# Weights of the dynamic convolution prepared in parts that fit the groups: what a new first part, new part borders and another order of the scratch rows do

## The chip, the cores and the metric

One NeuronCore of one Trainium2 chip runs the whole program. The metric is the device time of one execution in microseconds (us). The compute engines are named as in the profile: PE (TensorE), DVE (VectorE), ACT (ScalarE), POOL (GpSimd, which here mostly issues DMAs), and SP (SyncE, which only issues DMAs).

## The reference

```
# x [8, 4224, 192], weight_gen [8, 4224, 8 heads, 7 taps]; all float32
w   = softmax(weight_gen, axis=-1)                         # 7 weights for each row and head
y   = sum over k of w[b, s, h, k] * x_pad[b, s + k, h, :]  # 6 zero rows ahead of x, 24 channels a head
g   = sigmoid(sum over j of conv_w[j] * y_pad[:, s + j])   # depthwise convolution, 5 taps
out = (g * (y @ w_val)) @ w_out                            # 192 x 192 each
```

The first line of sums is a convolution whose weights differ for every row; the rest is a gated projection of its result.

## The kernel before

**Groups and pairs.** The 4224 rows of the sequence are cut into groups of 120 rows (the first has 88, the last 56). A group holds the rows of all 8 batch lanes. Pair 0 is the first group alone, pairs 1 to 17 are two groups each, pair 18 is the last group alone. Counting groups from 0, pair 1 is groups 1 and 2, pair 2 groups 3 and 4, pair 3 groups 5 and 6.

**The dynamic convolution as matmuls.** For a group, `bank` multiplies a tile `xt` (windows of 14 rows of x on the partitions) with a tile `tb`, in which the softmax weights stand as a band along a diagonal. There are two `tb` and three `xt` buffers, used in turn. The 128 PE instructions at line 343 are one group's band matmuls. ACT copies the result from PSUM (`evac`), and POOL moves pieces of it into the ring tiles by 12 small DMAs a pair (`move`).

**How the band gets into `tb`.** The softmax weights are computed in *parts* (class `Softmax`): a part of R rows per partition covers 32 R rows of all lanes. DVE and ACT run `max`, `sub`, `exp`, `sum`, `recip`, `norm` on it. `halo` then copies the 6 rows that follow each partition's own from a neighbour partition by DMA, `spread` (four copies) writes the weights in the form of band rows, and `store` writes these to a scratch buffer z in DRAM (two buffers, `zb`, used in turn). `load_t` reads z back with a row stride that is one step short, which puts the rows on a diagonal: nine DMAs for a group of 120 rows, one for each window of 14 rows. What a row of z holds outside its weights must be zero; `clear_z` writes those zeros.

**The gate and the projections.** `tap0` (ACT) and four `tap` for each of two channel groups (DVE, line 388) are the depthwise convolution; `sigm` (ACT), `wvm_`, `wva_`, `wvd_`, `wvb_` (PE) the value projection, `gv` (DVE, line 439 and on) the gating, `omA`, `omB` (PE) the output projection, `oev` (ACT) and `store` (SP) the output. On PE the band matmuls of pair q stand between the value projection of pair q-1 and the output projection of pair q-2. The band matmuls use PSUM tiles that `gv` of the pair before must first have read.

**What sets the order.** Every step is put into a list with a planned time (`at`); the list is sorted by that time and each engine gets its steps in that order. The planned times only order the steps. `WHEN` holds the planned starts of pairs 0 to 3, `TP` the planned distance of later pairs. Waits between engines are added from what each step reads and writes. A DMA on SP or ACT carries one of eight semaphores in turn, one on POOL one of eight others; a DMA waits until the one before it with the same semaphore has landed, so at most eight of each kind are under way.

**Parts before.** `USES` lists, for each of 11 parts, the first row for which it is used and its R:

```
USES = ((0, 4, NBL), (96, 10, NBL), (364, 8, NBL), (576, RM, NBL), (1070, RM, NBL), (1564, RM, NBL), (2058, RM, NBL),
        (2552, RM, NBL), (3046, RM, NBL), (3540, RM, NBL), (4034, 8, NBL))
```

The first part serves the first group, the second nearly all of pair 1. A group whose rows cross a border takes some windows from one part and the others from the next (`segments`).

## Time and profile before

| | |
|---|---|
| median of 3 runs (range) | 536.34 us (532.11 to 536.66) |
| the profiled execution: its own time | 530.59 us |
| its span, first to last instruction | 528.8 us |
| PE, DVE, ACT, POOL busy in the span | 454.5, 427.1, 313.6, 317.3 us |
| mean granted TensorE clock | 0.942 |
| DMA traffic | 112.42 MB, mean 213 GB/s |

The durations below come from the profiled execution; 1.79 us of its own time lie outside the span. Its own time is 5.75 us under the median of the three runs, so a sum made in the trace has to be moved by that much to stand beside the median. The first 110 us are start-up, in which PE mostly waits; after them PE is busy nearly without a break until the last two pairs.

### The profile page before, as it was taken

Reading aid. Unit: us, or ns where it says so; the run is one execution under the profiler, and the core shown is the slowest. Engines: PE = TensorE matmul, PEld = TensorE weight load, DVE = VectorE, ACT = ScalarE, POOL = GpSimd, SP = SyncE. Lnnn points to the kernel's source line nnn. Section 1 sums busy time; section 2 is a strip of 40 time slices with the busy share of each in tenths; the row PEclk is TensorE's granted clock in tenths of the full one; section 3 lists DMA queues with packets and bytes.
Section 4 is the critical chain, followed back from the end, with each engine's and each line's share of the span. In section 5 each row is a group of like instructions: output and inputs, shape, how many; then the busy total and the mean of one; then the engine's idle time right before and its main releaser. Section 6 shows DMA issues by size and latency. Waiting matters only on the chain.

```text
span 528.8 us, 15980 instructions
## 1 busy us (share of the span) xinstructions
PE 454.5 (86%) x6546; PEld 330.2 (62%) x6546; DVE 427.1 (81%) x342; ACT 313.6 (59%) x433; POOL 317.3 (60%) x554
## 2 busy tenths in 40 slices
PE   7030674969999899999999999999998999999996
PEld 3030552556858485858676776768584868586584
DVE  6988346898979896999799979888995979595960
ACT  6432364658585748485858675767767575545532
POOL 9878256667474839293949382938566565807400
PEclk9565697879999999999999999999999999999999
DMA  7796749986979797879797978797797858654344
GB/s 222 212 307 187 202 110 254 244 234 175 248 218 281 196 270 195 270 195 269 208 288 201 267 199 263 202 259 220 219 254 220 256 149 251 177 165 100 92 113 111
DMA packets 86743, 112.42 MB, mean 213 GB/s; under 512 B 19133, under 2 KB 73796, under 8 KB 86542
## 3 DMA queue, kind: packets, MB, share of 16 engines
q1 hardware_dynamic: 62988, 70.86, 46.9%
q0 software_dynamic: 22560, 38.13, 28.1%
q10 hardware_dynamic: 1122, 2.40, 1.4%
q8 instruction: 52, 0.85, 0.6%
q14 instruction: 21, 0.17, 0.1%
HBM read 59.63 MB, written 42.43 MB: 193 GB/s over the span
## 4 chain that ended last, share of the span: by engine, by line
PE 44%; issue 15%; DMA 14%; POOL 13%; DVE 7%; ACT 5%; SPq 2%; ACTq 0%; POOLq 0%; DVEq 0%
PE ps L343 15%; PE ps L455 10%; POOL xt L286 6%; PE ps L464 6%; PE ps L420 5%; POOL ringA L366 4%; DMA xt<-in_x_dram 3%; PE ps L415 3%; PE ps L432 3%; POOL ringB L368 2%; DMA ringA<-S 2%; DMA tb<-z 2%; DMA ringB<-S 2%; PE ps L426 2%; DVE aB L447 1%
## 5 line engine op out<-in xcount | busy, mean ns | idle before, releaser
L343 PE MATMUL ps<-tb,xt 126*32 126x120 f32 (+2 forms) x4608 | 148.0, 286 | 62.3 <-DMA tb<-z 26.8
L343 PEld LDWEIGHTS ps<-tb,xt 126*32 126x32 f32 x4608 | 134.9, 115 | 74.5 <-issue 33.4
L388 DVE SCALAR_TENSOR_TENSOR aA<-ringA,wf,aA 128x1920 f32<-128x1920 f32 (+2 forms) x76 | 157.3, 2070 | 15.9 <-ACT aA L384 13.7
L286 POOL DMA_DIRECT2D xt<-in_x_dram x272 | 158.4, 597 | 17.8 <-DMA xt<-in_x_dram 5.0
L368 POOL DMA_DIRECT2D ringB<-S x76 | 42.1, 559 | 139.0 <-ACT ringB L358 113.0
L455 PE MATMUL ps<-wf,aA 128*120 128x192 f32 (+2 forms) x576 | 108.7, 336 | 5.9 <-DVE aB L447 3.9
L455 PEld LDWEIGHTS ps<-wf,aA 128*120 128x120 f32 (+2 forms) x576 | 91.2, 186 | 20.2 <-DVE aB L447 9.0
L470 ACT COPY ot<-ps 120x768 f32<-120x768 f32 (+2 forms) x72 | 56.0, 802 | 66.2 <-PE ps L464 55.2
L366 POOL DMA_DIRECT2D ringA<-S x152 | 82.0, 547 | 21.6 <-DMA ringB<-S 9.0
L388 DVE SCALAR_TENSOR_TENSOR aB<-ringB,wf,aB 128x960 f32<-128x960 f32 (+2 forms) x76 | 86.9, 1143 | 1.9
L439 DVE TENSOR_TENSOR aA<-ps,aA 128x960 f32<-128x960 f32 (+2 forms) x36 | 39.3, 1130 | 52.7 <-PE ps L432 33.1
L420 PE MATMUL ps<-ringA,wva 128*128 128x480 f32 (+2 forms) x144 | 61.8, 571 | 0.0
L464 PE MATMUL ps<-wf,aB 64*120 64x192 f32 (+2 forms) x576 | 59.7, 335 | 0.9 <-ACT ot L470 0.9
L358 ACT COPY S<-ps 128x480 f32<-128x480 f32 (+2 forms) x36 | 19.9, 552 | 63.2 <-PE ps L343 46.5
L464 PEld LDWEIGHTS ps<-wf,aB 64*120 64x120 f32 (+2 forms) x576 | 46.5, 182 | 16.8 <-issue 15.2
L358 ACT COPY ringA<-ps 128x480 f32<-128x480 f32 (+2 forms) x72 | 36.2, 554 | 33.7 <-PE ps L343 33.7
L384 ACT ACTIVATE aA<-ringA,wf 128x960 f32<-128x960 f32 (+2 forms) x38 | 39.2, 1033 | 22.9 <-DMA ringA<-S 22.7
L420 PEld LDWEIGHTS ps<-ringA,wva 128*128 128x128 f32 x144 | 25.8, 189 | 35.7 <-issue 22.2
L261 ACT COPY zt<-wt 128x512 f32<-128x512 f32 (+3 forms) x36 | 30.9, 936 | 5.7 <-DMA wt<-wt 3.2
L432 PE MATMUL ps<-ringB,wvb 64*128 64x480 f32 (+2 forms) x144 | 33.5, 581 | 0.0
L415 PE MATMUL ps<-ringA,wvm 128*32 128x480 f32 (+2 forms) x304 | 33.5, 537 | 0.0
L393 ACT ACTIVATE aA<-aA 128x1920 f32<-128x1920 f32 (+2 forms) x19 | 32.1, 1690 | 1.0 <-DVE aA L388 0.9
(62 smaller groups left out, 361.1 us busy)
## 6 DMA issues: line engine op xcount, KB each, us to landing
xt<-in_x_dram POOLq DMA_DIRECT2D x272, 94.5 KB, 3.7
out_dram<-ot SPq DMA_DIRECT2D x68, 360.0 KB
tb<-z SPq DMA_DIRECT2D x235, 74.4 KB
z<-zt SPq DMA_DIRECT2D x28, 306.0 KB
wt<-in_weight_gen_dram SPq DMA_DIRECT2D x28, 224.0 KB
ringA<-S POOLq DMA_DIRECT2D x136, 30.0 KB, 3.5
tb<-z SPq DMA_DIRECT2D x69, 52.1 KB
wt<-wt SPq DMA_DIRECT2D x9, 294.0 KB
```

Source lines behind the costliest of these rows:

```text
L286: eng.dma_start(out=self.xb[0:G * NW, j, 0:D], in_=src)
L343: nc.tensor.matmul(out=pa[Q * c:Q * c + Q, n * l:n * l + n], lhsT=g.xb[0:k, LH * u + l, C * h:C * h + Q], rhs=t[:, (LH * u + l) // LQ, PAD ...
L358: nc.scalar.copy(out=dst, in_=pa)
L366: nc.gpsimd.dma_start(out=ringA[q:q + h, LH * u:LH * u + LH, p0:p0 + n], in_=St[p:p + h, :, 0:n])
L368: nc.gpsimd.dma_start(out=ringB[HD * u + q:HD * u + q + h, :, p0:p0 + n], in_=St[p:p + h, :, 0:n])
L388: nc.vector.scalar_tensor_tensor(out=a, in0=self.src(g, j), scalar=cw[:, g, j:j + 1], in1=a, op0=ALU.mult, op1=ALU.add)
L415: nc.tensor.matmul(out=ps[2][c:c + Q, i, 0:self.w * self.pieces // 2], lhsT=wvm[:, Q * k:Q * k + Q], rhs=self.half(0, u, i), start=True, s ...
L420: nc.tensor.matmul(out=self.v01(e)[:, u], lhsT=wva, rhs=self.A(e, u), start=True, stop=False)
L432: nc.tensor.matmul(out=self.v01(e)[:, u], lhsT=wvb[hs], rhs=self.Bt(e)[hs], start=False, stop=True, tile_position=(HD * u, 0))
L455: nc.tensor.matmul(out=ps[b][0:n, u, D * t:D * t + D], lhsT=g[:, u, t], rhs=woa, start=first and t == 0, stop=not first, skip_group_check= ...
L464: nc.tensor.matmul(out=ps[b][0:n, u, D * t:D * t + D], lhsT=g[hs, t], rhs=wob[hs], start=first and t == 0, stop=not first, skip_group_chec ...
L470: nc.scalar.copy(out=ots[0:n, 2 * e + k], in_=ps[b][0:n, :, 0:2 * D])
```

## The change

1. The first group has 80 rows and the last 64; groups between keep 120, and there are as many pairs.
2. The parts have other borders: `(0, 10), (314, 8), (554, 8)`, then seven parts of R = 16 that start at 794 and lie 480 apart, then `(4154, 6)`. Each but the first starts six rows (`PAD`) ahead of the first row of a pair, so both groups of a pair read one part, and `load_t` is issued by windows alone.
3. The first part now has R = 10 and reads its six following rows from DRAM itself, so that it needs no `halo`; it covers groups 0, 1 and 2. Its softmax is done in two halves of 8 rows per partition.
4. z holds for each row the band rows of the four lane pairs one after the other (before: all rows of a lane pair, then the next lane pair). `store` and `load_t` get other strides; the pieces that they move stay 612 bytes and up to 1360 bytes. A row that is stored is 612 bytes in all parts (before: the first two parts stored rows of 1428 bytes, zeros included).
5. `clear_z` zeroes only the 816 bytes behind the weights, in one DMA for all lanes; there are four such DMAs, all on SP.
6. The weights of a part are loaded by one DMA instead of four.
7. Of the copies of `spread`, DVE makes two in each of the first two parts. Conversions and DMAs of the projection weights come earlier.
8. The start-up table is written anew: groups 0, 1 and 2 follow each other on PE, `WHEN` is other, and `tap0` of pair 0 comes after the last `evac` of pair 1 on ACT.

```diff
-    N0, NZ = 88, 56
+    N0, NZ = 80, 64
...
-    def clear_z(i, lo, p, n, eng):
+    def clear_z(i, lo, hi, eng):
...
+        t, n = zb[i], NL * (hi - lo) // 16
+        dst = bass.AP(tensor=t.tensor, offset=t.offset + NL * lo * PITCH + DATA,
+                      ap=[[n * PITCH, 16], [PITCH, n], [1, PITCH - DATA]])
...
+        def load(self, eng, lo=0, hi=None):
+            R, n = self.R, (hi or self.m) - lo
+            src = bass.AP(tensor=wg.tensor, offset=wg.offset + (self.r0 + lo) * ROW,
+                          ap=[[R * ROW, NBL], [LQ * S * ROW, NL], [S * ROW, LQ], [1, n * ROW]])
...
-                dst = bass.AP(tensor=t.tensor, offset=t.offset + ROWS * u * PITCH,
-                              ap=[[R * PITCH, p], [PITCH, R], [1, self.row]])
+                dst = bass.AP(tensor=t.tensor, offset=t.offset + u * PITCH,
+                              ap=[[R * NL * PITCH, p], [NL * PITCH, R], [1, self.row]])
...
-            off = (self.s - PAD + lo - p.r0) * PITCH + HC2 + skip * CELL - HC2 * i0
+            off = (self.s - PAD + lo - p.r0) * NL * PITCH + HC2 + skip * CELL - HC2 * i0
             src = bass.AP(tensor=b.tensor, offset=b.offset + off,
-                          ap=[[PITCH - HC2, hi - lo], [ROWS * PITCH, NL], [1, cells * CELL]])
+                          ap=[[NL * PITCH - HC2, hi - lo], [PITCH, NL], [1, cells * CELL]])
...
+    USES = ((0, 10, NBL), (314, 8, NBL), (554, 8, NBL), *((794 + 480 * i, RM, NBL) for i in range(7)), (4154, 6, NBL))
...
-    WHEN = (25.0, 40.0, 52.0, 70.0)
+    WHEN = (25.0, 30.0, 54.0, 79.0)
...
+    steps(s0, "max sub exp", 4.1, *h0)
+    steps(s0, "max sub exp", 4.2, *h1)
+    steps(s0, "sum recip norm", 4.3, *h0)
+    steps(s0, "sum recip norm", 4.4, *h1)
...
+    at(29.5, s3.load, SP)
...
+    steps(s3, "max sub", 44.0)
+    spread(s2, 45.0)
...
+    at(46.9, s3.exp)
```

**DVE at the start.** First before, then now, with the semaphores that each step waits for; `wt_65` holds the weights of the first part, `mx_68` its maxima and sums, DMAHW names DMAs of SP and ACT.

```order
L215 TENSOR_REDUCE mx_68<-wt_65 128x160 [waits DMAHW2_49,DMAHW3_49,DMAHW1_49,DMAHW0_49]
L219 TENSOR_TENSOR wt_65<-wt_65,mx_68 128x1120 [waits DVE_49]
L227 TENSOR_REDUCE mx_68<-wt_65 128x160 [waits Activation_49]
L231 TENSOR_SCALAR mx_68<-mx_68 128x160 [waits DVE_49]
L232 RECIPROCAL mx_68<-mx_68 128x160 [waits DVE_49]
L249 TENSOR_TENSOR wt_65<-wt_65,mx_68 128x1120 [waits DVE_49]
L215 TENSOR_REDUCE mx_69<-wt_66 128x160 [waits DMAHW6_49,DMAHW5_49,DMAHW7_49,DMAHW4_49,Pool_49]
```

```order
L215 TENSOR_REDUCE mx_68<-wt_65 128x2x64 [waits DMAHW1_49,DMAHW0_49]
L219 TENSOR_TENSOR wt_65<-wt_65,mx_68 128x2x448 [waits DVE_49]
L215 TENSOR_REDUCE mx_68<-wt_65 128x2x64 [waits Activation_49]
L219 TENSOR_TENSOR wt_65<-wt_65,mx_68 128x2x448 [waits DVE_49]
L227 TENSOR_REDUCE mx_68<-wt_65 128x2x64 [waits Activation_49]
L231 TENSOR_SCALAR mx_68<-mx_68 128x2x64 [waits DVE_49]
L232 RECIPROCAL mx_68<-mx_68 128x2x64 [waits DVE_49]
L236 TENSOR_TENSOR wt_65<-wt_65,mx_68 128x2x448 [waits DVE_49]
```

The first step waits for the loads of both halves, and the second half's maximum waits for ACT, which at that point has only the first half's `exp` to finish.

**SP from the zeroing of z to the loads of the second group.** First before, then now; `z_97` and `z_98` are the two scratch buffers, `tb_64` and `tb_63` the band tiles of groups 0 and 1 (and `tb_64` again of group 2).

```order
L181 DMA z_97<-zero 128x1x357 x4
L272 DMA z_97<-aA 32x1428 x2
L317 DMA tb_64<-z_97 8x4x238
L317 DMA tb_64<-z_97 14x4x340 x2
L317 DMA tb_64<-z_97 10x4x170
L206 DMA wt_65<-in_weight_gen_dram 32x2x896 x4
L272 DMA z_98<-aA 32x3570 x2
L241 DMA wt_67<-wt_67 112x2x336
L241 DMA wt_67<-wt_67 12x2x336
L317 DMA tb_63<-z_97 14x4x238
L272 DMA z_97<-zt 256x1x153 x4
L317 DMA tb_63<-z_98 14x4x340 x3
```

```order
L180 DMA z_97<-zero 1280x1x204
L205 DMA wt_67<-in_weight_gen_dram 128x2x448
L180 DMA z_98<-zero 1024x1x204
L272 DMA z_97<-aA 320x1x153 x2
L313 DMA tb_64<-z_97 8x4x238
L313 DMA tb_64<-z_97 14x4x340 x2
L313 DMA tb_64<-z_97 2x4x34
L313 DMA tb_63<-z_97 14x4x238
L313 DMA tb_63<-z_97 14x4x340 x3
L313 DMA tb_63<-z_97 14x4x238
L272 DMA z_98<-aA 256x1x153 x4
```

Between the loads of group 0 and those of group 1 stood the load of the fourth part, the stores of the second and third and a halo; now nothing stands there, and the second part's store comes behind group 1's loads.

**SP ahead of the loads of pair 3** (its first group's are the last rows of each, into `tb_63`). First before, then now.

```order
L317 DMA tb_64<-z_97 14x4x238
L272 DMA z_98<-zt 512x1x153 x4
L206 DMA wt_66<-in_weight_gen_dram 32x2x896 x4
L478 DMA out_dram<-ot 44x2x384 x2
L317 DMA tb_63<-z_97 14x4x238
L317 DMA tb_63<-z_98 14x4x340 x7
L317 DMA tb_63<-z_98 14x4x238
```

```order
L205 DMA wt_66<-in_weight_gen_dram 128x2x896
L272 DMA z_97<-zt 256x1x153 x4
L180 DMA z_98<-zero 1024x1x204
L245 DMA wt_65<-wt_65 112x2x336
L245 DMA wt_65<-wt_65 12x2x336
L474 DMA out_dram<-ot 40x2x384 x2
L313 DMA tb_63<-z_97 14x4x238
L313 DMA tb_63<-z_97 14x4x340 x7
```

The two halo DMAs of the fourth part (`wt_65`) now stand ahead of pair 3's loads, and with them the wait for that part's `norm` on DVE; they stood far ahead of these before.

## Rows read from the trace of the kernel before

**Rows 1.** Windows, core 0: us, busy of PE, PEld, DVE, ACT, POOL, clock, DMA share, GB/s.

```profile
0.00:110.65 110.65, 50.83 (x787) 36.09 (x787) 78.77 (x83) 51.34 (x77) 76.71 (x129) 0.75 0.80 216
110.65:528.80 418.15, 403.66 (x5760) 294.14 (x5760) 348.33 (x260) 262.28 (x357) 240.62 (x425) 0.99 0.76 212
...
139.00:463.00 324.00, 314.51 (x4605) 228.64 (x4597) 282.34 (x204) 214.29 (x287) 201.13 (x356) 1.00 0.83 231
```

**Rows 2.** Timeline of PE, start-up: start, us, engine, line, operation; band matmuls of groups 0, 1, 3, 5.

```profile
29.74 4.65 PE L343 MATMUL ps<-tb,xt 126*32 126x88 f32 x128 [19.13 <-DMA ot<-cd]
56.34 5.98 PE L343 MATMUL ps<-tb,xt 126*32 126x120 f32 x128 [21.96 <-DMA tb<-z]
...
75.13 3.88 PE L343 MATMUL ps<-tb,xt 126*32 126x120 f32 x128 [1.11 <-DVE aA L439]
...
110.65 6.06 PE L343 MATMUL ps<-tb,xt 126*32 126x120 f32 x128 [4.81 <-DMA tb<-z]
```

**Rows 3.** Timeline of SP, start-up: loads of z, halo, output, loads of z.

```profile
21.55 3.44 SPq L317 DMA_DIRECT2D tb<-z  x4
...
57.06 4.04 SPq L241 DMA_DIRECT2D wt<-wt  x2
...
86.60 1.66 SPq L478 DMA_DIRECT2D out_dram<-ot  x2
...
89.36 20.68 SPq L317 DMA_DIRECT2D tb<-z  x18
```

**Rows 4.** Timeline of DVE, first 32 us: first part's first and last step, third part's tensor_scalar.

```profile
5.63 1.32 DVE L215 TENSOR_REDUCE mx<-wt 128x160 f32<-128x1120 f32 x1 [2.70 <-DMA wt<-in_weight_gen_dram]
...
12.33 1.32 DVE L249 TENSOR_TENSOR wt<-wt,mx 128x1120 f32<-128x1120 f32 x1
...
28.34 3.52 DVE L231 TENSOR_SCALAR mx<-mx 128x128 f32<-128x128 f32 x1
```

**Rows 5.** Groups by line and form, 0 to 110.6 us: softmax steps on 896 elements.

```profile
L219 DVE TENSOR_TENSOR wt<-wt,mx 128x896 f32<-128x896 f32 x1 | 1.1, 1086 | 0.0
...
L232 DVE RECIPROCAL mx<-mx 128x128 f32<-128x128 f32 x1 | 1.0, 952 | 0.0
L223 ACT ACTIVATE wt<-wt 128x896 f32<-128x896 f32 x1 | 0.9, 949 | 5.5 <-DMA tb<-z 5.5
```

**Rows 6.** Timeline of POOL, 27 to 32 us: memsets.

```profile
27.76 1.94 POOL L511 MEMSET tb<- 128x2142 f32 x1
29.58 2.20 POOL L578 MEMSET zt<- 128x2448 f32 x1
```

**Rows 7.** Timeline of ACT, 62 to 100 us: tap0 of pair 0, a spread, an exp.

```profile
62.82 1.06 ACT L384 ACTIVATE aA<-ringA,wf 128x352 f32<-128x352 f32 x2
...
64.39 3.85 ACT L261 COPY zt<-wt 128x512 f32<-128x512 f32 x4
...
97.00 1.28 ACT L223 ACT_TABLE_LOAD   x1
98.69 1.70 ACT L223 ACTIVATE wt<-wt 128x1792 f32<-128x1792 f32 x1 [0.40 <-DVE wt L219]
```

**Rows 8.** Timeline of DVE, 82 to 128 us: taps, a part's last steps, gating.

```profile
82.00 8.98 DVE L388 SCALAR_TENSOR_TENSOR aA<-ringA,wf,aA 128x1920 f32<-128x1920 f32 x4 [5.96 <-ACT aA L384]
...
102.21 2.01 DVE L227 TENSOR_REDUCE mx<-wt 128x256 f32<-128x1792 f32 x1
...
104.59 1.75 DVE L232 RECIPROCAL mx<-mx 128x256 f32<-128x256 f32 x1
106.37 2.02 DVE L249 TENSOR_TENSOR wt<-wt,mx 128x1792 f32<-128x1792 f32 x1
...
109.44 2.21 DVE L439 TENSOR_TENSOR aA<-ps,aA 128x960 f32<-128x960 f32 x2
...
122.51 4.97 DVE L388 SCALAR_TENSOR_TENSOR aB<-ringB,wf,aB 128x960 f32<-128x960 f32 x4
```

**Rows 9.** Timeline of PE: band matmuls of the last group.

```profile
489.56 1.96 PE L343 MATMUL ps<-tb,xt 126*32 126x56 f32 x128
```

More of the change, by code (lines that the diff above doesn't have):

```diff
@@ L547, in tile_dynconv_gated_moe @@
-    tail(s1, 1.1)
-    tail(s2, 1.1)
-    steps(s0, "max sub exp", 4.1)
-    at(4.5, lambda: A.copy(out=s1.z, in_=zero[:, 0:1].unsqueeze(2).broadcast_to([P, s1.R, PITCH])))
-    steps(s0, "sum recip norm", 5.0)
-    at(7.0, clear_z, 0, 128, 16, 8, SP)
-    steps(s1, "max sub", 8.3)
-    at(8.5, s2.max)
-    at(10.0, gr[1].load_x, G_)
-    spread(s0, 11.0)
-    at(11.1, s0.store, (A, SP))
-    at(12.1, s1.exp)
-    steps(s1, "sum recip norm", 12.2)
-    at(12.3, lambda: clear(tb[0], 0, 0, CELLS, A))
@@ L572, in tile_dynconv_gated_moe @@
-    at(19.6, lambda: clear(tb[0], 2, 0, CELLS, G_))
-    at(20.0, s1.halo, (G_, G_))
-    at(20.5, load_weights)
-    spread(s1, 24.0)
-    at(24.5, s1.store, (A, SP))
-    at(24.6, lambda: clear(tb[0], 3, 0, CELLS, G_))
-    at(24.7, lambda: G_.memset(zt, 0.0))
-    tail(s3, 24.8)
-    at(24.9, s2.halo, (SP,))
-    steps(s3, "max sub", 26.0)
-    at(28.4, s3.exp)
-    steps(s3, "sum recip norm", 28.5)
-    at(29.5, gr[2].load_x, G_)
-    spread(s2, 30.0)
-    at(31.0, s2.store, (SP,))
+    at(0.2, s1.load, SP)
@@ new lines, in tile_dynconv_gated_moe @@
+    at(5.5, clear_z, 1, 0, 256, SP)
+    steps(s0, "max sub exp", 4.1, *h0)
+    steps(s0, "max sub exp", 4.2, *h1)
+    steps(s0, "sum recip norm", 4.3, *h0)
+    steps(s0, "sum recip norm", 4.4, *h1)
+    tb_clear(1, 2, 8.0, A, 0, cs)
+    tb_clear(1, 3, 8.1, A, 0, cs)
+    spread(s0, 11.0, (A, V, A, V))
+    at(11.1, s0.store, (SP, A))
+    tb_clear(0, 2, 11.5, A)
+    steps(s1, "max sub exp", 12.0)
+    tb_clear(0, 3, 12.1, A)
+    for u in range(NL):
+        tb_clear(1, u, 12.05 if u < 2 else 12.3, V, cs)
@@ L593, in tile_dynconv_gated_moe @@
-    spread(s3, 43.0)
-    for i, f in enumerate(place_weights()):
-        at(44.0 + 0.01 * i, f)
-    at(43.5, clear_z, 1, 320, 16, 12, G_)
-    load(s4, 51.0, (SP,))
-    at(50.0, s3.store, (SP,))
-    s0.ready, s1.ready, s2.ready, s3.ready = 12.0, 24.5, 31.0, 50.5
-    at(54.0, clear_z, 0, 256, 16, 16, G_)
-    steps(s4, "max sub exp", 62.0)
-    steps(s4, "sum recip norm", 66.0)
-    for p in parts[3:]:
-        q = next(q.q for q in pairs if p.use < q.s + q.n)
-        if p is s3:
-            assert q == 3
-            continue
-        if p is not s4:
-            for u in range(NL):
-                at(when(q - 5) + 12.5, p.load, u, SP)
+            at((14.0, 28.0, 29.0)[k] + 0.01 * i, lambda f=f: f(V))
@@ new lines, in tile_dynconv_gated_moe @@
+    for gi, t in enumerate((20.5, 24.0, 29.0)):
+        for w, lo, hi in gr[gi].windows():
+            at(t + 0.01 * w, gr[gi].load_t, s0, w, lo, hi, (SP, A)[w % 2])
+    spread(s1, 24.9, (A, A, V, V))
+    at(28.5, s1.store, (SP,))
+    tail(s3, 26.0)
+    at(37.0, lambda: G_.memset(zt, 0.0))
+    at(29.5, s3.load, SP)
+    steps(s2, "max sub", 32.5)
+    for i, f in enumerate(place_weights()):
+        at(33.35 + 0.001 * i, f)
+    at(32.6, s2.exp)
+    steps(s2, "sum recip norm", 32.7)
+    at(33.0, s2.halo, (G_,))
@@ L612, in tile_dynconv_gated_moe @@
+    steps(s3, "max sub", 44.0)
+    spread(s2, 45.0)
+    at(46.0, s2.store, (SP,))
+    tail(parts[4], 46.5)
+    tail(parts[5], 46.6)
+    at(46.9, s3.exp)
+    at(47.0, clear_z, 1, 256, 512, SP)
+    at(when(3) + 7.5, clear_z, 0, 320, 512, SP)
+    steps(s3, "sum recip norm", when(1) + 20.6)
+    for p in parts[3:]:
+        q = part.index(p)
+        if p is not s3:
+            at(when(q - 5) + 12.5, p.load, SP)
             for i, f in enumerate((p.max, p.sub)):
@@ L618, in tile_dynconv_gated_moe @@
         spread(p, when(q - 2) + 8.0)
-        p.ready = when(q - 2) + 12.0
-        at(p.ready, p.store, (SP,))
+        at(when(q - 2) + 12.0, p.store, (SP,))
     for q, pr in enumerate(pairs + [None, None]):
```

175 lines of the change are left out of this document (79 added, 96 removed).

## The prediction

> **What bounds the kernel now.** I read the windows first. From 110.65 us to the end PE is busy 403.66 of 418.15 us at a granted clock of 0.99; up to there it is busy 50.83 of 110.65 [rows 1]. So from the first band matmul of group 5 (pair 3) on, PE sets the pace, and ahead of it something else does. Pair 3 starts at 110.65 and the last group's matmuls at 489.56 [rows 2, 9], fifteen pairs in 378.9 us, 25.3 us a pair, and nothing in the change takes work off PE there. What can move the end is the time T3 at which pair 3 starts on PE. The PE order up to that point is the same in both kernels, so what PE has left after T3 is the same too, but for the cut of the last group.
>
> The PE timeline then shows where the 110 us went: group 0 starts at 29.74, group 1 only at 56.34, group 3 at 75.13, group 5 at 110.65 [rows 2]. The waits stand at the row ends: group 1 waited 21.96 us for `tb<-z`, group 5 another 4.81 us. Start-up is a chain of softmax, store to z, load from z, matmul, paid for several small parts one after the other.
>
> **The change, part by part.** I follow the new chain with the old durations.
>
> *First part to group 0.* Before, DVE starts when 573 KB of weights have landed, at 5.63 [rows 4]. Now it waits for both halves, 917 KB; the extra 344 KB cost between nothing (the same row) and 1.6 us at the 216 GB/s of start-up [rows 1]: I take 6.5. The halves do not overlap, because DVE waits for ACT's `exp` between them (the order of the change shows it). `max` and `sub` cost 1.09 us each for 896 elements, `exp` 0.95 [rows 5]: 2 x 3.13 = 6.3, to 12.8. Then twice `sum` 1.09, the small tensor_scalar with its gap 0.37 (102.21 + 2.01 to 104.59), reciprocal 0.95, `norm` 1.09 [rows 5, 8]: 7.0, to 19.8. Before, the first part's `norm` ended at 13.65 and the first load of `tb` was issued at 21.55 [rows 3, 4], 7.9 us for spread, store and landing; the new store has 783 KB instead of 731 and two of its four copies on DVE, so I keep 7.9: 27.7. From that issue to group 0 on PE passed 8.19 us (21.55 to 29.74) over seven loads on two queues; there are seven now: **group 0 at 35.9**, 6.2 us later than before. The zeroing of z (1.0 and 0.8 MB) is issued ahead of this store on the same queue; all that DMA has to move by then is some 5.4 MB, 25 us at 216 GB/s, so it just fits under the 22 us of softmax and spread and the landing that follows; without that cover each MB costs 4.6 us. That is the largest unknown of this step: 0 to 4 us.
>
> *Groups 1 and 2.* They read the same part, so their loads follow directly. PE needs 4.65 x 80/88 = 4.2 for group 0, to 40.1. Group 1's nine loads go out on two queues behind group 0's and can all have landed some 5 us after group 0's (five issues at 0.86 each [rows 3], 4 more if the eight semaphores hold them up). I take **group 1 at 40.5**, 16 us ahead of before. A band of 120 rows takes 3.88 us at the high clock and 5.98 at the low one [rows 2]; I take 5.5, to 46. Group 2 reuses the tile that group 0 frees at 40.1: five issues, 4.3, and the 4.7 that lay between the last issue's end (24.99) and the matmul (29.74) [rows 2, 3]: 49.1, and 5 us of matmul, **to 54**.
>
> *Pair 2.* `tap0` of pair 0 now comes after all four `evac` of group 2 on ACT, which end 1 us after the matmuls, at 55. From that `tap0` to group 3 on PE passed 75.13 - 62.82 = 12.31 us, of which 3.85 were a `spread` that stood between [rows 2, 7]: 8.5 remain. **Group 3 at 63.5**, 11.6 ahead of before.
>
> *Pair 3.* `gv` of pair 0 takes DVE until 64.5, `max` and `sub` of the fourth part 2 x 2.02, to 68.6. ACT meanwhile has `tap0` of pair 1 (3.2), the third part's spread (2.4) and a table load of 1.28 [rows 7], and ends that part's `exp` (1.70) at 71.6. `sum` to `norm` take 102.21 to 108.39, 6.2 [rows 8]: 77.8. Only then come the taps of pair 1 on DVE, 8.98 and 4.97 [rows 8], to 91.7, and the first `gv`, half of 2.21, frees the PSUM tile that group 5 needs: 92.8. On SP the fourth part's halo waits for the same `norm`; behind it stand two halo issues (1.6 to 4.0), two output issues (1.66) and nine loads (18 took 20.68 with their waits, so 7.5 to 10.3) [rows 3], and some 3 us of landing: 91.6 to 96.8. Both chains end at the same place. I take **T3 = 93.0**, 17.7 ahead. By bytes the same comes out: the DMAs that must be through by then hold some 19.9 MB (summed over the new program's order), and 216 GB/s moves that in 92 us.
>
> *After T3.* The loads by one DMA instead of four take three issues off SP for every part, and a group no longer mixes parts; it had nine loads either way, since the old borders fell on window borders. SP waits were not what PE lost after 110.65, so I cost this at nothing; if I am wrong it can give back at most the 14.5 us that PE was idle there [rows 1]. The last group of 64 rows instead of 56 costs 1.96 x 8/56 = 0.3 in band matmuls [rows 9] and about as much in its projections: 0.6.
>
> *A rule of the skill that speaks against it.* The third part's tensor_scalar took 3.52 us where the same step elsewhere takes 0.3, while POOL's memsets ran from 27.76 to 31.78 [rows 4, 6]. The Trainium skill, SBUF — State Buffer, Who interferes with whom, says that a VectorE copy or tensor_scalar in a two-port mode and a GpSimd operation lock each other out for a whole instruction; this row agrees. By that rule the spread copies now on DVE could hold up POOL's DMA issues, and POOL's early memsets the new half-size tensor_scalars. In the sum above POOL's last early memset ends near 12, 3 us ahead of the first tensor_scalar, so the sum has nothing for it; by the rule with both halves hit it would be 6 us more.
>
> *Sum.* 528.8 - 17.7 + 0.6 = 511.7 in the span, with 1.79 around it 513.5. The profiled execution lies 5.75 us under the median of its runs, so beside that median I say **519 us**.
>
> **Rivals.** *(a) Start-up is as short as the new plan writes it:* pair 3 at 79. For it: PE is idle for more than half of the old start-up and DVE for 32 of its 110 us [rows 1]. Against: the old plan said 70 and got 110.65, and the DVE chain alone adds up to 93. It would need the taps of pair 1 ahead of the fourth part's `exp`. It gives 14 us less: 505.
> *(b) The gain is eaten on the way:* group 3 and the fourth part are late because start-up's DMA is the bound and the four zeroing DMAs, now ahead of loads on one queue, stand in the way. 23.9 MB were moved by 110.65, and if as much must be moved now, T3 falls back to 105 or more: 531 to 537, no change. Against: the DMA share of start-up was 0.80, not full [rows 1], and the bytes counted are 4 MB fewer.
> *(c) Slower:* the new order of z makes each z transfer dearer in every pair, since rows that one store writes now lie 5712 bytes apart instead of 1428. A pair moves 1.3 MB out of z and 0.6 into it, of some 5.7 MB, a third; DMA is at 0.83 of the time [rows 1], 21 of 25.3 us. The pieces may cost 1.6 times as much before a pair's DMA fills its 25.3 us; at double it would be 28, 2.8 us more in 15 pairs, 42, less 17.7: 560. Against: pieces keep their size, and the lanes of a row now lie side by side. It decides from 1.8 times on, where the start-up gain is gone.
> *(d) The halves overlap after all,* or the first part lands early: 3 to 5 us better, inside the range.
>
> **How the numbers follow.** The forecast with T3 between 88 and 99 (and up to 4 us either way after it) has a chance of 0.66: 513 to 526. (a), including a steady part that loses less idle time, has 0.16 (500 to 512), (b) 0.12, (c) 0.06. The range leaves out the slow half of (b), (c) and the best of (a): **507 to 530**. What a measurement can tell from no change is about 1% here, 531 to 541.7: faster 0.84 (the forecast, (a), and a little of (b)), within 0.10, slower 0.06.
>
> **What would show it.** Group 0 on PE at 36, later than before; groups 1 and 2 at about 40 and 49; group 3 at 63; group 5 at 93 with DVE's taps of pair 1 directly ahead of `gv` and no idle time in between; after it 25 us a pair and a DMA share near 0.83. The prediction is wrong if group 0 starts after 42 (the zeroing stands ahead of the first store), if PE waits for `tb<-z` or `xt` at pairs 4 to 17, or if pairs take over 26 us.

## The result and the profile after

The changed kernel takes 530.66 us (median of 20 runs, 524.48 to 536.48), the kernel before 535.19 in the same runs (median of 20, 532.11 to 539.3). The ratio is 0.9876, 95% interval 0.9847 to 0.9906: 1.2% faster, about 6.6 us, where 17 had been forecast. The ratio sets the mean of the fast runs of each kernel side by side, 528.85 us (14 of the 20) and 535.47 (all 20); the six slower runs of the changed kernel are not in it, which is why it is lower than that of the two medians. The profiled execution after has a span of 529.9 (531.67 with what lies around it), near its median; that of before lay 4.6 under its own, so the two spans, 528.8 and 529.9, don't show the gain. It also means that the 5.75 us by which the forecast was moved, taken from three runs, were 4.6 by the twenty.

Windows of the changed kernel, to be held against [rows 1] (us; busy time of PE, PEld, DVE, ACT, POOL; granted clock; DMA share; GB/s); the last one is ten microseconds in pair 4:

```profile
0.00:98.64 98.64, 49.90 (x786) 36.80 (x787) 68.37 (x86) 50.21 (x75) 78.03 (x132) 0.74 0.84 217
98.64:529.90 431.26, 407.38 (x5760) 298.11 (x5760) 357.49 (x266) 264.64 (x360) 234.83 (x415) 0.99 0.76 208
139.00:463.00 324.00, 308.20 (x4374) 224.15 (x4371) 277.87 (x203) 211.30 (x282) 199.69 (x354) 0.99 0.82 226
150.00:160.00 10.00, 9.06 (x100) 8.39 (x104) 9.87 (x8) 4.92 (x6) 4.73 (x9) 0.66 0.96 246
```

Start-up lasts 98.64 us instead of 110.65, but what follows takes 431.26 instead of 418.15, for the same 5760 matmuls. From 139 to 463 PE is busy for 6.3 us less than before, and 231 fewer matmuls lie in that stretch.

Part of the shorter start-up is work that now stands behind it. DVE has six instructions and 9.2 us more to do from pair 3's start on than before (266 and 357.49 us, against 260 and 348.33 in [rows 1]), and the DMA engines, by rate times length, about 1 MB more (89.7 against 88.6). The six are the steps of the fifth part's softmax. Before, its `norm` ended at 108.39, ahead of pair 3 [rows 8]; now it stands here:

```profile
128.80 2.02 DVE L236 TENSOR_TENSOR wt<-wt,mx 128x1792 f32<-128x1792 f32 x1
```

So the lead at pair 3 is not all work saved. What this part costs behind pair 3 no run tells by itself.

Timeline of PE in start-up, after, to be held against [rows 2]: band matmuls of groups 0, 1, 2, 3 and 5.

```profile
37.15 4.22 PE L339 MATMUL ps<-tb,xt 126*32 126x80 f32 x128 [26.48 <-DMA xt<-in_x_dram]
43.70 5.32 PE L339 MATMUL ps<-tb,xt 126*32 126x120 f32 x128 [2.33 <-DMA z<-aA]
51.43 5.22 PE L339 MATMUL ps<-tb,xt 126*32 126x120 f32 x128 [2.41 <-DMA tb<-z]
...
65.38 5.04 PE L339 MATMUL ps<-tb,xt 126*32 126x120 f32 x128 [5.74 <-DMA ringA<-S]
...
98.64 3.63 PE L339 MATMUL ps<-tb,xt 126*32 126x120 f32 x68 [5.32 <-DMA tb<-z]
```

The forecast had 35.9, 40.5, 49.1, 63.5 and 93.0. The order is as forecast, the first four groups are 1.3 to 3.2 us late, and pair 3 is 5.6 us late.

To follow the lead past pair 3 I take the first `evac` of pairs 3, 6, 16 and of the last group (timeline of ACT). First the kernel before, then the changed one:

```profile
114.14 0.56 ACT L358 COPY S<-ps 128x480 f32<-128x480 f32 x1 [1.90 <-PE ps L343]
190.73 0.56 ACT L358 COPY S<-ps 128x480 f32<-128x480 f32 x1 [1.13 <-PE ps L343]
442.72 0.56 ACT L358 COPY S<-ps 128x480 f32<-128x480 f32 x1 [1.13 <-PE ps L343]
490.71 0.35 ACT L358 COPY S<-ps 128x224 f32<-128x224 f32 x1 [0.17 <-PE ps L343]
```

```profile
102.13 0.56 ACT L354 COPY S<-ps 128x480 f32<-128x480 f32 x1 [1.51 <-PE ps L339]
184.62 0.56 ACT L354 COPY S<-ps 128x480 f32<-128x480 f32 x1 [1.13 <-PE ps L339]
442.69 0.56 ACT L354 COPY S<-ps 128x480 f32<-128x480 f32 x1 [1.13 <-PE ps L339]
491.18 0.38 ACT L354 COPY S<-ps 128x256 f32<-128x256 f32 x1 [0.29 <-PE ps L339]
```

The lead is 12.0 us at pair 3, 6.1 at pair 6, nothing at pair 16. So two things are to be explained: 5.6 us in start-up, and a loss of 5.9 us in pairs 3 to 6 and 6.1 in pairs 6 to 16. In the spans of these two executions they are nearly all of what is missing: 17.1 us less had been forecast and 1.1 more came. By the ratio 10.5 us are missing, because this execution of the kernel before was a short one.

Pair 3 is already longer. It takes 27.6 us from its first `evac` to that of pair 4 (102.13 to 129.69), against 25.1 before (114.14 to 139.25); in the second traces of both (`d_after` and `d_old_spread`, below) it is 27.6 against 25.2. ACT and PE of the changed kernel there:

```profile
120.51 1.09 ACT L380 ACTIVATE aA<-ringA,wf 128x960 f32<-128x960 f32 x1 [2.88 <-DMA ringA<-S]
```

```profile
124.58 1.57 PE L451 MATMUL ps<-wf,aA 128*120 128x192 f32 x8 [1.98 <-DVE aB L443]
```

PE waits for the last `gv` on DVE, this for the second `sigm` on ACT, and that stands behind a `tap0` that waits 2.9 us for the ring moves (0.5 us before). The ring moves are issued 10.3 us after the pair's first `evac` instead of 8.3; what POOL waits for the profile does not name. A second chain ends close by: DVE works without a pause from 96.8 to 121.0, with `max` and `sub` of the fifth part (4.1 us) ahead of the taps, where before it was idle for 2.5 us ahead of `gv`. In `c_spread` and `d_spread` (below) `tap0` waits only 0.4 and 0.6 us there, PE waits 2.9 us for `gv` on `aA` instead, and pair 3 still takes 27.6. No run took both chains away.

The next suspect was pair 4. Four timelines of the changed kernel there, SP, ACT, DVE and PE in this order:

```profile
127.90 0.57 SPq L180 DMA_DIRECT2D z<-zero  x1
128.59 0.69 SPq L205 DMA_DIRECT2D wt<-in_weight_gen_dram  x1
129.37 5.30 SPq L474 DMA_DIRECT2D out_dram<-ot  x3
134.77 2.32 SPq L245 DMA_DIRECT2D wt<-wt  x2
```

```profile
143.16 3.76 ACT L261 COPY zt<-wt 128x512 f32<-128x512 f32 x4 [4.33 <-DMA tb<-z]
146.83 1.80 ACT L389 ACTIVATE aA<-aA 128x1920 f32<-128x1920 f32 x1
```

```profile
148.66 2.22 DVE L435 TENSOR_TENSOR aA<-ps,aA 128x960 f32<-128x960 f32 x2 [4.05 <-ACT aA L389]
```

```profile
150.94 1.32 PE L451 MATMUL ps<-wf,aA 128*120 128x192 f32 x3 [3.22 <-DVE aA L435]
```

Read upward from PE: it waits 3.2 us for `gv` on DVE, which waits for `sigm` on ACT, which stands behind `spread`, which waits 4.3 us for a transfer. What `spread` reads is the part's halo (`wt<-wt`), issued at 134.77 behind zeroes, 896 KB of weights and three output stores. Pair 4 takes 30.5 us, against 25.1 before (27.4 against 24.8 in the second traces). After its wait PE runs at a granted clock of 0.66 (the window above), part of the time at the lower of its two levels. The same wait of `spread`, 4.2 us, stands once more at 249.

### The profile page after: what moved, and what is told of

Read it like the earlier page. It is cut to its first block, busy times and chain, and to the rows that moved or that the text cites. A ratio compares the mean times of both kernels' runs of the same rounds, so it can differ in the third digit from the quotient of the medians.

```text
span 529.9 us, 15947 instructions
## 1 busy us (share of the span) xinstructions
PE 457.3 (86%) x6546; PEld 334.9 (63%) x6546; DVE 425.9 (80%) x351; ACT 314.8 (59%) x434; POOL 312.9 (59%) x546
## 4 chain that ended last, share of the span: by engine, by line
PE 31%; issue 21%; POOL 18%; DMA 13%; DVE 9%; ACT 7%; POOLq 0%; ACTq 0%; DVEq 0%
PE ps L339 11%; PE ps L451 8%; POOL xt L286 8%; PE ps L460 5%; DMA ringA<-S 5%; POOL ringA L362 5%; POOL ringB L364 4%; DMA xt<-in_x_dram 4%; DVE aA L435 3%; PE ps L416 3%; DVE aB L443 3%; ACT aA L389 2%; DVE aA L384 2%; PE ps L411 1%; DMA wt<-wt 1%
## 5 line engine op out<-in xcount | busy, mean ns | idle before, releaser
L339 PE MATMUL ps<-tb,xt 126*32 126x120 f32 (+2 forms) x4608 | 148.0, 287 | 52.1 <-DMA xt<-in_x_dram 26.5
L339 PEld LDWEIGHTS ps<-tb,xt 126*32 126x32 f32 x4608 | 136.3, 115 | 62.7 <-issue 41.9
L451 PE MATMUL ps<-wf,aA 128*120 128x192 f32 (+2 forms) x576 | 111.6, 342 | 14.1 <-DVE aA L435 7.0
L451 PEld LDWEIGHTS ps<-wf,aA 128*120 128x120 f32 (+2 forms) x576 | 93.5, 190 | 28.8 <-DVE aB L443 11.6
L460 PEld LDWEIGHTS ps<-wf,aB 64*120 64x120 f32 (+2 forms) x576 | 46.8, 183 | 17.1 <-issue 15.4
L261 ACT COPY zt<-wt 128x512 f32<-128x512 f32 (+4 forms) x36 | 30.3, 920 | 15.8 <-DMA tb<-z 8.5
```

Source lines behind the costliest of these rows:

```text
L339: nc.tensor.matmul(out=pa[Q * c:Q * c + Q, n * l:n * l + n], lhsT=g.xb[0:k, LH * u + l, C * h:C * h + Q], rhs=t[:, (LH * u + l) // LQ, PAD ...
L451: nc.tensor.matmul(out=ps[b][0:n, u, D * t:D * t + D], lhsT=g[:, u, t], rhs=woa, start=first and t == 0, stop=not first, skip_group_check= ...
L460: nc.tensor.matmul(out=ps[b][0:n, u, D * t:D * t + D], lhsT=g[hs, t], rhs=wob[hs], start=first and t == 0, stop=not first, skip_group_chec ...
```

## The experiments

Theories, as the expectations name them. **A**: PE's own work sets the pace after pair 3; a few early waits cost the lead. **B**: the DMA engines set it, so a lead is worth nothing. **C**: transfers crowd just after pair 3. **D**: the late halo, through `spread`, `sigm` and `gv`. **E**: PE and DMA are both nearly full, a wait that is removed comes back elsewhere. **F**: the chain through DVE sets the pace. Ratios are to the kernel before, run beside; the changed kernel itself has 0.9876.

**1. A lead made smaller** (`a_delay`).

```diff
+        if q == 3:
+            st(-0.001, stir, 40)
```

> The changed kernel with 40 more of the start-up's stir matmuls on PE directly ahead of the band matmuls of pair 3. Each took 0.40 us at the low clock and should take 0.20 at the high one, so pair 3 starts 8 to 14 us later (107 to 113 instead of 98.6), while no DMA is added. Theory A, PE's own work sets the pace after pair 3 and the lead was lost to a few early waits: the end moves by at least 4 us, 535 to 542, ratio to the kernel before 0.997 to 1.01. Theory B, the DMA engines set the pace after pair 3 and a lead at pair 3 is worth nothing: the delay is worth nothing either, 530 to 532, ratio 0.985 to 0.992.

Measured 1.0014 (0.9983 to 1.0044), 534.46 us. PE there:

```profile
95.88 8.46 PE L480 MATMUL ps<-zero 128*128 128x368 bf16 x40 [6.71 <-DVE aA L435]
104.27 3.88 PE L339 MATMUL ps<-tb,xt 126*32 126x120 f32 x128
```

The first evac of pair 3 comes at 106.37, that of the last group at 493.91; in the changed kernel's second trace (`d_after`, below) at 101.95 and 489.28. The delay came out smaller than expected: the 40 matmuls took 0.21 us each, not up to 0.40, which was the mean length of overlapping ones. A delay of 4.4 us at pair 3 is still 4.6 at the end (4.2 and 2.7 against the first trace; by the ratios it is 7 us). Pairs 3 to 16 take 339.7 us, in `d_after` 339.5. **B falls**: time at pair 3 reaches the end, and the changed kernel must be losing its lead by pairs that are longer in themselves.

**2 to 5. Less work in pairs 6 to 15** (`a_nomb`, `a_nostore`, `b_both`, `e_notap`).

```diff
 a_nomb, b_both:    -  st(tB[i], p2.omB, ...)            for 6 <= q < 16
 a_nostore, b_both: -  st(tE[i] + 0.01, p2.store, ...)   for 6 <= q < 16
 e_notap:           -  the tap 0, KC - 1                 for 6 <= q < 16
```

> The changed kernel without the second half of the output projection (omB) in pairs 6 to 15 (their outputs miss the terms of the second ring), 3.1 us of PE matmuls a pair, 31 us in all, and no DMA less. Theory A (PE's own work sets the pace): 24 to 31 us less, 500 to 507, ratio 0.93 to 0.945. Theory B (DMA sets the pace): PE just waits longer, 526 to 531, ratio 0.98 to 0.99. In between: DVE, ACT or DMA are the next bound close behind PE.

> The changed kernel without the stores of the output of pairs 6 to 15 (their rows of the output are left unwritten), some 14.7 MB less of 111, 15 us of all 16 DMA engines a pair down by a quarter. Theory A (PE's own work sets the pace after pair 3): only the idle time of PE from 200 to 463 us can go, 11.4 us in the profiled execution, and of it the part that late transfers cause: 522 to 530, ratio 0.975 to 0.988. Theory B (DMA sets the pace): all of that idle time goes and pairs 6 to 15 run at PE's 24.2 us: 518 to 521, ratio 0.965 to 0.972.

> The changed kernel without omB and without the output stores in pairs 6 to 15 (those outputs are not written). Each alone gave little: without omB 0.982, without the stores 0.9885, against 0.9876 for the change itself. Theory E (PE with 24.3 us a pair and DMA with some 24.5 us both limit): together they free the pairs down to DVE's 22 us, 500 to 510, ratio 0.935 to 0.955. Theory D alone (waits for halos set the pace whatever the load): still above 518, 0.970 or more.

> The changed kernel without the last tap on the first ring in pairs 6 to 15 (their outputs miss that term): 2.2 us less of DVE a pair, 22 us in all, nothing less on PE and DMA. Without omB (31 us of PE) the kernel gained 3 us, without stores (14.7 MB) nothing, without both 13 us. Theory F (a pair is a chain of evac, ring moves, tap0, taps, sigm, gv through ACT, DVE and DMA, and this chain sets the pace): shorter by 2.2 us a pair, 508 to 516, ratio 0.95 to 0.966. Theory E (PE and DMA are the two limits, DVE is not): at most 3 us, 0.981 to 0.989.

Measured: without `omB` 0.9818 (0.9756 to 0.988); without the stores 0.9885 (0.9843 to 0.9927); without both 0.9627 (0.9579 to 0.9675), 516.64 us; without the tap 0.9881 (0.9842 to 0.9921). The windows from 200 to 463 us of the four, in this order:

```profile
200.00:463.00 263.00, 235.62 (x3375) 163.53 (x3373) 230.33 (x169) 176.59 (x237) 166.81 (x295) 0.98 0.84 228
```

```profile
200.00:463.00 263.00, 254.20 (x3742) 187.35 (x3745) 229.74 (x166) 172.88 (x232) 160.85 (x284) 0.99 0.71 181
```

```profile
200.00:463.00 263.00, 239.74 (x3628) 172.53 (x3628) 235.97 (x171) 178.24 (x242) 163.50 (x290) 0.99 0.72 184
```

```profile
200.00:463.00 263.00, 252.02 (x3661) 183.35 (x3663) 204.33 (x154) 169.74 (x229) 159.28 (x283) 0.99 0.83 226
```

Less work of one kind gave little: 31 us of PE matmuls some 3 us (0 to 6 by the interval), 14.7 MB of transfers nothing beyond the interval of 2 us, and 22 us of DVE the same. PE and DMA together gave 13. **A and F fall**, and E's size with them (it expected 500 to 510): neither PE nor DMA alone sets the pace, both together do in part.

**6. Stores of pairs 1 to 4 alone** (`a_nostore_early`: the same edit for 1 <= q < 5).

> The changed kernel without the stores of the output of pairs 1 to 4 alone (left unwritten), 5.9 MB less between 100 and 200 us. Theory C, a local debt: after pair 3 the ring moves, x loads, the zeroing of z and the stores crowd there, which cost PE 7.3 us of waits from 98.6 to 200 and 2 us at a lower granted clock; with the stores gone 4 to 8 us of it come back and are kept to the end: 522 to 527, ratio 0.974 to 0.983. Theory B (DMA sets the pace all along): the lead gained here melts later, 528 to 531, ratio 0.984 to 0.990. If the waits of pairs 4 and 5 come from the order on DVE and ACT and not from DMA, nothing changes either, and then PE still waits for gv at about 121 and 151 us.

Measured 0.9825 (0.9763 to 0.9888). In its trace the first evacs of pairs 3 and 6 lie 81.0 us apart, as in the changed kernel (82.5, and 80.2 in `d_after`). So pairs 3 to 6 are as long without the crowd of stores; the half per cent is inside the intervals.

**7, 8. The load and the halo behind it** (`b_late`, `b_load4`).

```diff
 b_late:
-            at(when(q - 5) + 12.5, p.load, SP)
+            at(when(q - 4) + 9.0, p.load, SP)
 b_load4:
+            for u in range(NL):
+                at(when(q - 5) + 12.5, p.load_u, u, SP)
```

> The changed kernel with each later part's weights load (896 KB, one DMA) moved on SP from ahead of the previous part's halo to behind the next tb loads. Theory D: the lead is lost where ACT's spread waits for the halo, which is queued behind that load (4.3 us at 143, 4.2 at 249), so that sigm and gv come late, PE waits about 3 us and then runs at a low granted clock (0.66 from 150 to 160). Then pairs 4 to 5 take 25 instead of 30.5 us, the 28 us pair goes too, and the end comes 6 to 12 us earlier: 519 to 525, ratio 0.967 to 0.978. Theory E (PE and the DMA engines are both so nearly full that any wait removed comes back as another): 527 to 531, 0.982 to 0.990.

> The changed kernel with each later part's weights loaded by four DMAs of 224 KB, one a lane pair, as before, instead of one of 896 KB; the place on SP is unchanged. If the single large DMA is what holds up the halo behind it: the long waits of spread (143, 249) shrink to the 2.6 us of before and 4 to 8 us come back, 522 to 527, ratio 0.975 to 0.983. If the bytes ahead of the halo hold it up and not their form: unchanged, 529 to 532, ratio 0.984 to 0.991.

`b_late` measured 1.0649 (1.0601 to 1.0698), 572.34 us. On DVE and, for pairs 6 to 9, on ACT:

```profile
171.85 2.02 DVE L215 TENSOR_REDUCE mx<-wt 128x256 f32<-128x1792 f32 x1 [13.38 <-DMA wt<-in_weight_gen_dram]
```

```profile
200.78 0.57 ACT L354 COPY S<-ps 128x480 f32<-128x480 f32 x1 [1.13 <-PE ps L339]
225.13 0.56 ACT L354 COPY S<-ps 128x480 f32<-128x480 f32 x1 [1.13 <-PE ps L339]
259.14 0.56 ACT L354 COPY S<-ps 128x480 f32<-128x480 f32 x1 [1.13 <-PE ps L339]
```

My edit brought a wait of its own: the load came so late that DVE's `max` stood 7 to 13 us and held up every second pair (34.0 from 225.13 to 259.14). The pairs in which the halo goes out took 24.35 (200.78 to 225.13), less than any such pair of the changed kernel. That is what a pair takes when PE waits for nothing: it is busy for 24.31 of the 24.35 us. `b_load4` measured 0.9877 (0.9835 to 0.9918): one load DMA instead of four costs and gains nothing beyond that interval.

**9. The old row order of z** (`a_oldz`: `store`, `load_t` and `clear_z` with a lane's rows together, all else as changed).

> The changed kernel with the z rows laid out as before, a lane's rows together, all else as changed. The traced DMA time of the two kernels' large queue was 267 against 256 engine-us. If the new row order makes z transfers dearer in every pair and that is what eats the lead: 3 to 6 us less, 524.5 to 528, ratio 0.976 to 0.983. If the row order does nothing for the time: 529 to 532, ratio 0.984 to 0.991; if lanes side by side help: more, from 0.993 on.

Measured 1.0468 (1.0414 to 1.0522), 561.57 us, outside all that was expected. Most of the loss lies in start-up: the first `evac` of pair 3 comes at 128.12, 26 us later. The first row is PE's first group there. The next two are the DMA issues on SP directly behind the first and the second zeroing. The last two are the DMA queue of SP (packets, MB, share of 16 engines' span), in this kernel and in the changed one:

```profile
54.47 4.49 PE L339 MATMUL ps<-tb,xt 126*32 126x80 f32 x128 [44.57 <-DVE wf L139]
```

```profile
3.58 19.06 SPq L205 DMA_DIRECT2D wt<-in_weight_gen_dram  x1
...
25.37 16.87 SPq L272 DMA_DIRECT2D z<-aA  x2
```

```profile
q1 hardware_dynamic: 67468, 73.14, 46.2%
```

```profile
q1 hardware_dynamic: 67516, 73.14, 49.3%
```

In the changed kernel these issues took 4.74 us (at 3.55) and 1.22 (at 21.03). SP is so held up by 14 us ahead of the first store to z, where this kernel differs from the changed one in nothing but the form of the zeroing, and by another 16 at that store. That form, across four lanes, makes at least the first of the two. Pair 3 starts at 124.6, and at 176.7 `spread` waits 13.0 us for a transfer; whether the order of the rows adds to that is not shown. The question that it was run for is answered by the later pairs: the queue's time is 0.462 x 561.9 = 259.6 us against 0.493 x 529.9 = 261.2, and pairs 6 to 16 take 255.9 us, against 258.1 and 259.3 for the changed kernel and 252.0 and 254.1 for the one before. Rival (c), dearer z transfers, is out as a doubling; 2 to 3 us of the loss may be its, which is less than the scatter of such a stretch (see below).

**10 to 14. The waits of spread** (`c_early`, `c_spread`, `e_clear`), **and the order ahead of pair 3** (`c_t3`, and `c_best` with `c_early` on top).

```diff
 c_early:
+            at(when(max(q - 6, 1)) + 12.5, p.load, SP)
 c_spread (the store follows at + 12.4; e_clear: and z0's last zeroing at when(4) + 13.0):
-        spread(p, when(q - 2) + 8.0)
+        spread(p, when(q - 2) + 12.0)
...
 c_t3:
-    steps(s3, "sum recip norm", when(1) + 20.6)
+    steps(s3, "sum recip norm", when(2) + 10.0)
+        d = (10.1, 31.6, 31.7) if p is s3 else (3.3, 8.0, 12.0)
...
+                    st((3.5 if q != 3 else 6.9, 7.0)[gi] + 0.001 * w, g.load_t, part[q + 1], w, lo, hi, SP)
...
-    at(33.0, s2.halo, (G_,))
+    at(36.9, s2.halo, (G_,))
```

> The changed kernel with each weights load from the sixth part on moved one pair forward on SP, behind the z store of that pair, so that no load stands directly ahead of a halo (the fifth part's stays). With the load behind the halo instead of ahead of it the pairs that took 30.5 and 28 us took 24.34, but DVE's max then waited 7 to 13 us for the load. Theory D (the halo behind the 896 KB load delays spread, then sigm, gv and PE): those waits go without a new one, pairs 4 and 8 take 25 to 26 us, the end is at 519 to 525, ratio 0.968 to 0.980. Theory E (PE and DMA both nearly full, a wait removed comes back elsewhere): 528 to 532, ratio 0.983 to 0.991.

> The changed kernel with the spread of each later part moved on ACT from ahead of the previous pair's first sigm to behind it (and its store behind that); the halo still waits behind the load. Theory D: what the late halo costs comes through ACT's order, so sigm, gv and PE no longer wait for it: 521 to 527, ratio 0.971 to 0.983, and the waits of PE for gv at about 151 and 257 us shrink from 3 us to under 1. If the second sigm and tap0 behind it take over the wait, or z is then stored too late for the tb loads: 529 to 540, ratio 0.985 to 1.005.

> The changed kernel with another order up to pair 3 only: the fourth part's sum to norm stand on DVE between the taps of pair 1 instead of ahead of them, where DVE waited 6.6 us for ACT's exp; its halo stands on SP behind the tb loads of pair 3, its spread on ACT behind the evac of pair 3; the third part's halo stands on POOL behind the ring moves of pair 1. Pair 3 should start on PE at 90 to 94 instead of 98.6. If a lead at pair 3 is kept to the end: 522 to 527, ratio 0.975 to 0.982. If it is given back by the DMA engines or by other waits, as most of the lead of the change was: 529 to 532, ratio 0.984 to 0.991.

> Both of the two edits before it together. If leads are kept and the halo waits are what lost them: 513 to 520, ratio 0.955 to 0.969. If PE and DMA are both so full that neither is kept: 528 to 532.

> The spread behind the first sigm, and the last zeroing of z0 (612 KB, issued at 127.9 in the first trace, ahead of a load and the fifth part's halo) one pair later, behind that pair's z store. Theory C (a local debt of transfers after pair 3 costs the first pairs): pairs 3 to 6, which took 79.5 us against 74.8 without the change, get 2 to 4 us back and keep them, 520 to 526, ratio 0.972 to 0.982. Theory E (given back elsewhere): as with the spread alone, 0.9835, within 0.980 to 0.988.

Measured: `c_early` 0.9866 (0.9827 to 0.9905), `c_spread` 0.9836 (0.9791 to 0.9881), `e_clear` 0.9884 (0.9818 to 0.995), `c_t3` 1.0106 (1.007 to 1.0142), `c_best` 1.0099 (1.0064 to 1.0134). The waits of ACT for transfers ahead of `spread`, from 98 to 463 us (total, times, longest), in the changed kernel (`d_after`), in `e_clear` and in `c_early`:

```profile
ACT zt L261 <- DMA tb<-z: 11.7, 4, 3.3
```

```profile
ACT zt L261 <- DMA wt<-wt: 0.2, 1, 0.2
```

```profile
ACT zt L261 <- DMA out_dram<-ot: 2.7, 1, 2.7
```

Two edits take the waits away, `e_clear` by the place of `spread` and `c_early` by that of the load (the 2.7 us left are those of the fifth part, whose load stays), and the time is what it was. **D is a true mechanism with next to no price**: the stall at 143 can be seen and removed, and pairs 6 to 16 of `e_clear` still take 257.7 us. The wait comes back in another place: from pair 6 to 16 PE waits 4.7 us for `gv` on `aA` and 1.8 for `gv` on `aB` in `d_after`, and 8.8 for `gv` on `aB` alone in `d_spread`. Where the stall stood a part of it stays gone: pairs 3 to 6 take 77.6, 79.5 and 78.5 us in `c_spread`, `d_spread` and `e_clear`, against 82.5 and 80.2, but 82.2 in `d_best`, which has the edit too.

`c_t3` did what it was to do at pair 3 and lost more behind it. PE there:

```profile
90.20 3.87 PE L339 MATMUL ps<-tb,xt 126*32 126x120 f32 x128 [1.66 <-DVE aA L435]
...
129.18 1.22 PE L339 MATMUL ps<-tb,xt 126*32 126x120 f32 x19 [5.11 <-DMA tb<-z]
```

Pair 3 starts 8.4 us earlier, but the fourth part, whose steps I had put back for it, now brings pair 4's band matmuls late: its store to z is issued at 110.28, the loads that need it (which the edit also put later, the line with `load_t` above) from 119.52 on, and PE waits for `tb<-z` until 129.18.

**15 to 18. The changed kernel again, and the spread edit on both kernels** (`d_after`, `d_spread`, `d_old_spread`; `d_best` has the third part's halo behind pair 1's ring moves on POOL and the fourth part's `exp` ahead of a spread on ACT besides).

> The changed kernel itself, again, as the neighbour of the other three on the same chip, and as a second trace of it. If what its first trace shows is its rule and not chance, spread waits about 4 us for the halo of the fifth part (pair 4) and once more later, pair 4 to 5 takes 28.5 to 31 us, and the ratio is 0.984 to 0.991.

> The spread behind the first sigm, once more (0.9836, interval 0.979 to 0.988, against 0.9876 for the change in other runs). Theory D: 3 to 6 us under the changed kernel on the same chip, ratio 0.977 to 0.983. Theory E: within 2 us of it, 0.984 to 0.990.

> The kernel before, with the same edit (the spread of the later parts on ACT behind the first sigm, the store behind it). Its trace had one wait of 2.6 us of spread for the halo (at 176), and PE waited 1.5 us for gv behind that. Theory D (the halo waits are what the change added, and ate its lead): nearly nothing here, 0 to 2 us, ratio 0.996 to 1.002. If the edit helps the kernel before as much as the changed one (0.990 or less), the halo waits are a cost of both and don't tell where the lead went.

> The changed kernel with the spread behind the first sigm and two edits ahead of pair 3: the third part's halo on POOL behind the ring moves of pair 1 (which waited 3.1 us for it), and the fourth part's exp on ACT ahead of the third part's spread, so that sum to norm, its halo and its z come earlier too, unlike in the run that put them later. Pair 3 at 92 to 96 on PE instead of 98.6. If a lead is kept once the halo waits are out of sigm's way: 514 to 520 where the changed kernel takes 530, ratio 0.965 to 0.978. If leads are given back all the same: as with the spread alone, 0.980 to 0.988.

Measured: 0.9877 (0.9814 to 0.994), 0.9835 (0.9776 to 0.9895), 0.9983 (0.9943 to 1.0023) and 0.987 (0.9829 to 0.991). The edit does nothing for the kernel before, so its trace can stand as a second one of it. First evacs again (pairs 3, 6, 16, last group), first `d_old_spread`, then `d_after`:

```profile
116.77 0.56 ACT L358 COPY S<-ps 128x480 f32<-128x480 f32 x1 [1.91 <-PE ps L343]
191.59 0.56 ACT L358 COPY S<-ps 128x480 f32<-128x480 f32 x1 [1.13 <-PE ps L343]
445.68 0.57 ACT L358 COPY S<-ps 128x480 f32<-128x480 f32 x1 [1.11 <-PE ps L343]
494.75 0.35 ACT L358 COPY S<-ps 128x224 f32<-128x224 f32 x1 [0.16 <-PE ps L343]
```

```profile
101.95 0.56 ACT L354 COPY S<-ps 128x480 f32<-128x480 f32 x1 [0.91 <-PE ps L339]
182.14 0.56 ACT L354 COPY S<-ps 128x480 f32<-128x480 f32 x1 [1.13 <-PE ps L339]
441.45 0.56 ACT L354 COPY S<-ps 128x480 f32<-128x480 f32 x1 [1.13 <-PE ps L339]
489.28 0.37 ACT L354 COPY S<-ps 128x256 f32<-128x256 f32 x1 [0.26 <-PE ps L339]
```

The lead is 14.8, 9.5, 4.2 and 5.5 us. Pairs 3 to 6 take 80.2 us against 74.8 (82.5 against 76.6 in the first traces), pairs 6 to 16 take 259.3 against 254.1 (258.1 against 252.0). Two traces each agree on a loss of some 5.5 us in either stretch. Three more traces, in which pairs 6 to 16 do the work of the changed kernel, bear the second out: 258.3 us in `a_delay`, 258.0 in `a_nostore_early`, 258.5 in `b_load4`. `d_best` has pair 3 at 98.13, no earlier, so it says nothing on leads: PE waited for `tb<-z` there with DVE's `gv` done, the second of the two chains that the prediction had seen end together.

## Why the prediction was wrong

The sign, the start-up walk and the place of the gain were right; the size was not, 6.6 us instead of 17.1. One sign that the prediction had named for being wrong came: seven of the pairs 3 to 15 took over 26 us from first `evac` to first `evac`, 30.5 the longest (before: four, 26.5 the longest).

**The step that failed** is "After T3 ... I cost this at nothing", with its ground, "PE sets the pace" from pair 3 on. I had read that ground from a busy share of 0.97 [rows 1]. The step asked only what could still be won behind T3, not what could be lost, and the chances gave that stretch 4 us either way. Taking 31 us of PE work out of ten pairs gave 3 us, so PE did not set the pace alone. The Trainium skill, Perfetto Trace Analysis, Identifying the Most-Contended Engine, says that matmul busy time is a bad measure of how near TensorE is to its limit, and that MFU and the busy share of weight loads are to be read instead. This case does not show that the second would have warned me: it was 0.71 in [rows 1] (228.64 of 324), and it is 0.73 (17.82 us) in the pair of `b_late` in which PE waits for nothing. That pair takes 24.35 us; the average is 25.2 to 26, and the rest are short waits, some of which came back in another place when one was removed. Against a forecast of nothing, the changed kernel's pairs 3 to 16 measured 10.6 to 12 us longer than those of before. The sentence "what PE has left after T3 is the same too" holds for PE, but not for DVE, which has a part's softmax more left.

That a head start at pair 3 shifts the end was right in itself: the delay of run 1 was still 2.7 to 4.6 of its 4.2 to 4.4 us at the end. What was wrong is that pairs behind T3 keep their length under the change.

**T3 was mis-sized**: 98.64 instead of 93.0, though within the 88 to 99 that the chances allow. Group 2 was 2.3 us late (51.43 instead of 49.1). The third part's halo on POOL held up pair 1's ring moves (3.1 us), `tap0` followed, and the fourth part's `exp` ended at 76.9 instead of 71.6. On DVE `sum` then waited, and all behind it had the forecast durations, the taps 8.97 and 4.98 us:

```profile
76.93 2.02 DVE L227 TENSOR_REDUCE mx<-wt 128x256 f32<-128x1792 f32 x1 [6.58 <-ACT wt L223]
...
96.83 2.21 DVE L435 TENSOR_TENSOR aA<-ps,aA 128x960 f32<-128x960 f32 x2
```

The change had put that halo on POOL instead of SP, and the prediction never looked at what stands behind it there. That this alone made T3 late is not shown: PE's wait ended with `tb<-z`, 0.7 us after the first of these `gv`, and in `d_best`, where that `gv` ends 2.4 us earlier, PE still waits for `tb<-z` until 98.13. The prediction had put that second chain, on SP, at 91.6 to 96.8.

**The rivals.** (a) fell: pair 3 at 98.6. (b) gave 531 to 537, near what came, but by a place where it did not happen: it needed pair 3 at 105 or later. (c) fell as a doubling. (d) did not show. Lane order aside, no rival had the loss where it was, in pairs 3 to 16. The long tensor_scalar beside POOL's work, which I had weighed, did not come either: those of the softmax steps in start-up took 0.23 to 0.29 us in this execution.

**What stays open** is why the pairs got longer. Not it, within 2 to 3 us each: the form of the load, the stores of pairs 1 to 4, and, for pairs 6 to 16, the halo waits and DVE's load. Of the loss in pairs 3 to 6, some 2.5 us lie in pair 3, behind the ring moves and DVE's extra part, and the rest about where pair 4 waits for its halo; the waits were followed through the traces, but no run prices those of pair 3. Possible for 2 to 3 us: the row order. Two traces of the same kernel, `c_spread` and `d_spread`, differ by 7 us in pairs 6 to 16 (253.1 and 260.0, with medians of 531.2 and 535.9 for the kernel before beside them), so single traces don't settle what is smaller than that.

Of the kernels that do all the work, the spread behind `sigm` has the lowest ratio, 0.9836 and 0.9835 in two runs; with other edits on top it has 0.9884 (`e_clear`) and 0.987 (`d_best`). It beats the kernel before, but is not shown to beat the changed one.
